# Rank and place of a step's 32 response products in the merged stage of a state-space and spectral mix

## The chip, the cores and the metric

The kernel runs on one core of one Trainium2 chip, as one launch. The metric is the time of the device in microseconds (us); lower is better. Five engines work side by side, each through its own instructions in a fixed order: TensorE (PE in the profile, its weight loads apart as PEld), VectorE (DVE), ScalarE (ACT), GpSimd (POOL) and SyncE (SP, which here only issues DMAs). An engine waits for another by semaphores, and an instruction that waits holds up all that stand behind it on its engine.

## The reference

Two branches work on one input `u` of 2048 positions and 640 channels, and a gate mixes them:

```python
def _A_ref(u, log_A_real, A_imag, C_real, C_imag, log_dt, D_skip):
    P = jnp.exp((A * dt[:, None])[:, :, None] * pos[None, None, :])
    K = 2.0 * jnp.einsum("dn,dnl->dl", C, P).real
    Kf = jnp.fft.rfft(K, L2)
    Uf = jnp.fft.rfft(u_t, L2)
    y = jnp.fft.irfft(Uf * Kf[None, :, :], L2)[:, :, :L]
    return y + u * D_skip[None, None, :]
def _B_ref(x, w_r, w_i):
    X = rfft2(x, axes=(-2, -1)) * (w_r + 1j * w_i)
    return irfft2(X, s=(S, D), axes=(-2, -1))
g = _sigmoid((x * gate_w).sum(-1, keepdims=True))
return g * a + (1 - g) * b
```

Branch a convolves each channel with a response `K` that is a sum over 128 complex modes of exp(pos x mode). Branch b is a filter in the two-dimensional spectrum.

## The kernel before

**Stages.** Every Fourier transform is done by matrix products with tables. In `body`, two streams of code are merged. The first, `ga`, is `phase_a` and the start of `phase_c`: the transform of `u` (products `p_s` in lines 372 and 385, copied out to tiles `t` and `ut`), then the spectral filter of branch b, a pipeline over nine blocks with transposes `p_t` (L557), products `p_d` (L573, L574), elementwise work on DVE (`xx`, `mm`, `zz`, `pm`, `ff`, L580 to L606), products `p_eo` (L618, L619) and `p_i` (L633). The second, `gl`, is `phase_p` and `phase_b`, which build the responses `K`. After both, `phase_d` convolves, gates and stores.

**The responses.** `phase_b` has 40 steps `t`, in batches of five. A position is split into two digits, so that a step's response is a product of two factors `x` and `y`, each a magnitude times a sine or cosine:
- `mags(t)`: three products `p_e` (L700) and three exponentials on ACT (L702) give the magnitudes. The five steps of a batch do this together, because the exponential and the sine each need their own table on ACT.
- `phases(t)`: two PSUM banks of three bf16 products each, `p_p` (L710), give the phases. The tiles of `p_e` and `p_p` share two banks.
- `trig(t)`: one absolute value on DVE (`aq`, L720) and five activations on ACT (L723 to L727) give `sc`, `sx` and `cx`. `sx` and `cx` have one buffer each.
- `prods(t)`: three instructions on DVE write `x` (L734, L735, L736), two on POOL write `y` (L739, L740). `x` and `y` have three buffers each.
- `kgen(t)`: the 32 response products `p_k` (L753), 128 x 32 weights by 128 x 64 columns in fp32, four of them side by side in the array. Each is two matmuls in the trace. After two steps ACT copies the bank to `kt` (L759), and after ten SP stores `kt` to the tensor `k_d` (L761), from which `phase_c` and `phase_d` load it again.

In the code `kgen(t - 3)` comes after `phases(t)` and `trig(t)`, except at the batch's edges, where `kgen` stands between the magnitudes of the next batch:

```python
            if len(pend) > 2:
                yield from kgen(pend.pop(0))
```

**What sets the order.** A scheduler places all instructions, engine by engine, before the run. An instruction's rank is the place at which the code reached it (the two streams are merged by estimated costs), and among the instructions that the scheduler takes to be ready, the one with the best rank is placed. Products of low rank thus fall into the places where others are not yet ready. `tc.issue_after(i)` adds a constraint of order alone: what is traced inside stands behind `i` on `i`'s engine.

## Time and profile before

| what | value |
|---|---|
| median of 3 runs | 561.67 us (560.4 to 561.99) |
| profiled execution, time | 560.56 us |
| its span | 558.8 us |
| PE, DVE, ACT, POOL busy | 516.2, 447.5, 339.8, 273.9 us |
| granted TensorE clock, mean | 0.984 |
| first and last response product | 79.0 and 395.1 us |
| response products' union on PE | 55.5 us of 2560 matmuls |

The responses lie in the stretch from 79 to 395 us, beside the work of the other stream. What counts in a table by stretches is which engine has no idle time left there: only work that leaves that engine can shorten the stretch.

### The profile page before, as it was taken

The numbers are of one execution on the slowest core, as the hardware profiler recorded it, in microseconds if no ns is written. First come the engines' busy times: TensorE is split into PE (matmuls) and PEld (weight loads), VectorE is DVE, ScalarE is ACT, GpSimd is POOL, SyncE is SP. The second block draws the span as 40 slices with busy tenths as digits, with TensorE's granted clock in tenths as the row PEclk, the third lists the DMA queues.
The fourth block names the chain that finished last, engine by engine and source line by source line (L and its number), as shares of the span: only waits on it lengthen the run. The fifth ranks groups of instructions, "written<-read, shape, count | busy, mean of one in ns | idle before, by whom it ended". The sixth has DMA issues, their size and how long they took to land.

```text
span 558.8 us, 16697 instructions
## 1 busy us (share of the span) xinstructions
PE 516.2 (92%) x7124; PEld 394.9 (71%) x7152; DVE 447.5 (80%) x684; ACT 339.8 (61%) x626; POOL 273.9 (49%) x277
## 2 busy tenths in 40 slices
PE   8899899997989899998999989999799999999975
PEld 6789456665857576867777766767787887787741
DVE  5997279479799979999979979876296885977945
ACT  4674677585587689797899786898224223241210
POOL 4993254056246327346257546165163446648433
PEclk9999999999899999999999999999899999999979
DMA  8969233165250331353222132115958989899877
GB/s 322 373 203 347 95 111 110 21 234 187 64 197 17 129 123 60 81 166 128 79 60 71 49 81 95 54 49 190 390 210 267 347 285 354 281 294 316 259 237 265
DMA packets 47697, 100.61 MB, mean 180 GB/s; under 512 B 3492, under 2 KB 32952, under 8 KB 45960
## 3 DMA queue, kind: packets, MB, share of 16 engines
q1 hardware_dynamic: 25176, 67.41, 34.7%
q10 hardware_dynamic: 20080, 22.52, 12.4%
q0 software_dynamic: 2368, 9.64, 5.1%
q8 instruction: 56, 0.92, 0.7%
q14 instruction: 17, 0.14, 0.1%
HBM read 60.22 MB, written 39.65 MB: 179 GB/s over the span
## 4 chain that ended last, share of the span: by engine, by line
PE 37%; DVE 6%; DMA 3%; ACT 3%; issue 1%; ACTq 0%; DVEq 0%; POOL 0%; SPq 0%
PE p_s L372 6%; PE p_s L385 6%; PE p_i L893 5%; PE p_e L172 3%; PE p_p L710 2%; PE p_k L753 2%; PE p_c L972 2%; DMA s_d<-s 2%; PE p_e L700 2%; PE p_i L633 2%; PE p_t L557 2%; PE p_eo L618 2%; PE p_eo L619 1%; PE p_d L573 1%; PE p_d L574 1%
## 5 line engine op out<-in xcount | busy, mean ns | idle before, releaser
L385 PE MATMUL p_s<-t,w 128*64 128x160 f32 x1056 | 90.5, 308 | 4.7 <-ACT ut L420 2.3
L385 PEld LDWEIGHTS p_s<-t,w 128*64 128x64 f32 x1056 | 75.4, 136 | 15.3 <-issue 4.3
L739 POOL TENSOR_TENSOR y<-e,sc 128x512 f32<-128x512 f32 x40 | 53.5, 1339 | 57.3 <-ACT sc L724 42.6
L702 ACT ACTIVATE e<-p_e 128x512 f32<-128x512 f32 x120 | 69.2, 608 | 14.0 <-PE p_e L700 12.7
L710 PE MATMUL p_p<-rp,par 128*128 128x512 bf16 x212 | 63.0, 380 | 8.1 <-ACT sx L726 4.5
L373 ACT COPY t<-p_s 128x512 f32<-128x512 f32 x40 | 24.8, 623 | 63.6 <-PE p_s L372 46.8
L753 PEld LDWEIGHTS p_k<-x,y 128*32 128x32 f32 x2560 | 42.2, 109 | 25.1 <-issue 20.7
L753 PE MATMUL p_k<-x,y 128*32 128x64 f32 x2560 | 55.5, 222 | 0.9 <-DVE x L735 0.8
L740 POOL TENSOR_TENSOR y<-e,sc 128x512 f32<-128x512 f32 x40 | 53.7, 1342 | 0.0
L700 PE MATMUL p_e<-rm,par 96*128 96x512 bf16 x120 | 43.4, 383 | 7.6 <-ACT e L702 4.3
L862 DVE TENSOR_TENSOR ma<-p_s,us 128x640 f32<-128x640 f32 (+1 forms) x36 | 28.2, 783 | 27.7 <-issue 22.0
L736 DVE TENSOR_TENSOR x<-e,cx 128x1024 f32<-128x1024 f32 x40 | 48.4, 1209 | 0.0
L372 PEld LDWEIGHTS p_s<-c,kt 128*64 128x64 f32 x640 | 39.2, 139 | 12.6 <-issue 7.1
L372 PE MATMUL p_s<-c,kt 128*64 128x128 f32 x640 | 44.6, 278 | 3.4 <-issue 2.2
L893 PE MATMUL p_i<-t,w 128*64 128x160 f32 x528 | 43.6, 306 | 3.9 <-POOL t L868 3.6
L895 ACT COPY s<-p_i 128x640 f32<-128x640 f32 x32 | 21.7, 694 | 38.7 <-PE p_i L893 23.4
L868 POOL TENSOR_TENSOR t<-mb 64x320 f32<-64x320 f32 (+1 forms) x36 | 29.9, 832 | 30.5 <-DVE t L868 30.1
L893 PEld LDWEIGHTS p_i<-t,w 128*64 128x64 f32 x528 | 37.4, 139 | 8.8 <-POOL t L868 4.3
L868 POOL TENSOR_TENSOR t<-ma 64x320 f32<-64x320 f32 x32 | 28.3, 886 | 29.9 <-DVE ma L862 28.7
L372 PE MATMUL p_s<-c,u 128*64 128x128 f32 x640 | 40.3, 276 | 0.8 <-ACT ut L420 0.6
L372 PEld LDWEIGHTS p_s<-c,u 128*64 128x64 f32 x640 | 35.3, 136 | 7.4 <-issue 5.3
L710 PEld LDWEIGHTS <-par 128*128 128x128 bf16 x240 | 21.3, 97 | 25.9 <-issue 12.0
(164 smaller groups left out, 1172.6 us busy)
## 6 DMA issues: line engine op xcount, KB each, us to landing
u_d<-ut SPq DMA_DIRECT2D x32, 320.0 KB, 2.8
us<-u_d ACTq DMA_DIRECT2D x16, 640.0 KB, 6.2
s_d<-s ACTq DMA_DIRECT2D x15, 640.0 KB, 9.2
t<-s_d SPq DMA_DIRECT2D x14, 640.0 KB, 6.8
ww<-in_w_l SPq DMA_DIRECT2D x8, 642.0 KB, 5.1
ue<-u_d SPq DMA_DIRECT2D x8, 640.0 KB, 4.2
k_d<-kt SPq DMA_DIRECT2D x4, 1280.0 KB, 4.5
kt<-k_d SPq DMA_DIRECT2D x8, 640.0 KB, 5.6
```

Of the source, the lines that this page charges most:

```text
L372: nc.tensor.matmul(p[64 * ri:64 * ri + 64, j, :], src(i + j), e1[ri], start=True, stop=True)
L385: ins = nc.tensor.matmul(p[64 * j:64 * j + 64, i, 160 * ri:160 * ri + 160], w2[:, x, 64 * ri:64 * ri + 64], t1[:, x // 2 if x < 32 else K0 ...
L700: P.matmul(p[:, :], pars[1][t], rm[:, c:c + 512], start=True, stop=True)
L702: st.exp = S.activation(ef[:, c:c + 512], p[:, :], AF.Exp)
L710: P.matmul(p[:, :], pars[0][t], w, start=i == 0, stop=i == 2)
L736: V.tensor_tensor(out=x[:, 0].rearrange("p d (h j) -> p d h j", h=2), in0=e[:, :, 0:64].rearrange("p d (h j) -> p d h j", h=2), in1=cx.uns ...
L739: G.tensor_tensor(out=y[:, 1], in0=e[:, :, 64:96], in1=sc[:, 0], op=ALU.mult)
L740: G.tensor_tensor(out=y[:, 0], in0=e[:, :, 64:96], in1=sc[:, 1], op=ALU.mult)
L753: P.matmul(st.pb[32 * r:32 * r + 32, o, :], y[:, ri, 4 * qq + JR[r], :], x[:, ri, 4 * qq + JR[r], :], start=t % 2 + qq + 1 - ri == 0, stop ...
L862: V.tensor_tensor(out=ma[:nl, :hn], in0=pv, in1=uu, op=ALU.mult)
L868: return eng.tensor_tensor(out=t2[64 * im:64 * im + 64, o, :], in0=m[l, :hn, 0, :], in1=m[l, :hn, 1, :], op=ALU.add if im else ALU.subtract)
L893: T.mm = P.matmul(p[x:x + 64, i // 2, 160 * (i % 2):160 * (i % 2) + 160], T.w3[:, k0 + h + i, x:x + 64], t2[:, h + i, :], start=True, stop ...
```

## The change

The response products are now placed under two conditions. They stand behind the latest phase product that the code has reached (`st.pp`, by `issue_after`), and their rank is raised by 200 places. Nothing is computed in another way, and no instruction is added or removed.

```diff
@@ phases(t, r)
-                P.matmul(p[:, :], pars[0][t], w, start=i == 0, stop=i == 2)
+                st.pp = P.matmul(p[:, :], pars[0][t], w, start=i == 0, stop=i == 2)
@@ kgen(t)
-        for qq in range(4):
-            o = 4 * (t % 2) + qq
-            for ri in (1, 0):
-                for r in (0, 1, 2, 3):
-                    P.matmul(st.pb[32 * r:32 * r + 32, o, :], y[:, ri, 4 * qq + JR[r], :], x[:, ri, 4 * qq + JR[r], :],
-                             start=t % 2 + qq + 1 - ri == 0, stop=t % 2 * qq == 3 and ri == 0)
+        with after(st.pp), tc.high_priority(offset=200):
+            for qq in range(4):
+                o = 4 * (t % 2) + qq
+                for ri in (1, 0):
+                    for r in (0, 1, 2, 3):
+                        P.matmul(st.pb[32 * r:32 * r + 32, o, :], y[:, ri, 4 * qq + JR[r], :], x[:, ri, 4 * qq + JR[r], :],
+                                 start=t % 2 + qq + 1 - ri == 0, stop=t % 2 * qq == 3 and ri == 0)
```

Below, a run is a row of response products that nothing else interrupts on PE. There are 83 runs before and 37 after; 24 of the 37 hold exactly one step's 32 products. By stretches of the span before, the runs are:

| stretch, us | steps whose products lie there | runs before | runs after |
|---|---|---|---|
| 72 to 111 | 0 to 3 | 14 | 4 |
| 111 to 135 | 4 to 8 | 11 | 4 |
| 158 to 205 | 9 to 13, before also a part of 14 | 11 | 6 |
| 205 to 244 | 14 to 18 | 8 | 4 |
| 244 to 271 | 19 to 23 | 8 | 6 |
| 271 to 323 | 24 to 28 | 12 | 4 |
| 323 to 353 | 29 to 33 | 8 | 5 |
| 353 to 396 | 34 to 39 | 11 | 4 |

On PE, at the end of the first batch (from the last phase product of step 4 on; the rows hold the end of step 1, step 2 and in the second list step 3), before:

```order
L710 MATMUL p_p<-rp,par_526 128x512
L753 MATMUL p_k<-x,y 32x64 x3
L385 MATMUL p_s_1248<-t_805,w_69 64x160 x4
L385 MATMUL p_s_1309<-t_805,w_69 64x160 x2
L372 MATMUL p_s_1315<-c_66,u 64x128 x8
L700 LDWEIGHTS par_1036
L700 MATMUL p_e<-rm,par_1036 128x512
L372 MATMUL p_s_1337<-c_66,u 64x128 x8
L753 MATMUL p_k<-x,y 32x64 x13
```

and now:

```order
L710 MATMUL p_p<-rp,par_526 128x512
L754 MATMUL p_k<-x,y 32x64 x32
L385 MATMUL p_s_1248<-t_805,w_69 64x160 x4
L385 MATMUL p_s_1309<-t_805,w_69 64x160 x2
L754 MATMUL p_k<-x,y 32x64 x36
L372 MATMUL p_s_1315<-c_66,u 64x128 x3
L754 MATMUL p_k<-x,y 32x64 x28
L372 MATMUL p_s_1315<-c_66,u 64x128 x5
```

Steps 2 and 3 moved ahead of the transform's products and of the next batch's magnitudes, and none of step 1 now stands ahead of the phase product.

On PE, in the fifth batch (from the last phase product of step 24 on; `p_k` are here the products of steps 21, 22 and 23, `p_d` those of the filter), before:

```order
L710 MATMUL p_p<-rp,par_2831 128x512
L753 MATMUL p_k<-x,y 32x64 x3
L574 MATMUL p_d<-td,ft 128x161
L573 MATMUL p_d<-td,ft 128x160
L574 MATMUL p_d<-td,ft 128x160
L753 MATMUL p_k<-x,y 32x64 x29
L573 MATMUL p_d<-td,ft 128x161
L574 MATMUL p_d<-td,ft 128x161
L573 MATMUL p_d<-td,ft 128x160
```

and now:

```order
L710 MATMUL p_p<-rp,par_2831 128x512
L754 MATMUL p_k<-x,y 32x64 x32
L573 MATMUL p_d<-td,ft 128x160
L574 MATMUL p_d<-td,ft 128x160
L573 MATMUL p_d<-td,ft 128x161
L754 MATMUL p_k<-x,y 32x64 x32
L574 MATMUL p_d<-td,ft 128x161
L573 MATMUL p_d<-td,ft 128x160
L754 MATMUL p_k<-x,y 32x64 x4
L574 MATMUL p_d<-td,ft 128x160
```

Before, steps 22 and 23 came behind all 16 `p_d` of the block; now 22 comes behind the fifth and the first four products of 23 behind the seventh.

On SP, at the end of the merged stage (`kt` are the responses loaded again, `k_d` the store of the last ten steps, `t3e` the result of the spectral filter, `w_5290` the table `T.w3` that `phase_d` needs for `p_i`), before:

```order
L809 DMA kt<-k_d 128x1280 x3
L1016 DMA w_5290<-in_t_w 128x1408 x3
L761 DMA k_d<-kt 128x2560
L809 DMA kt<-k_d 128x1280
L933 DMA t3e<-s3e_d 128x2560
```

and now:

```order
L810 DMA kt<-k_d 128x1280 x2
L762 DMA k_d<-kt 128x2560
L810 DMA kt<-k_d 128x1280 x2
L934 DMA t3e<-s3e_d 128x2560
L1017 DMA w_5290<-in_t_w 128x1408 x3
```

The store of the responses moved ahead of the third load, and the table's three loads moved behind the fourth `kt` and behind `t3e`. On ACT, the copy of a finished pair of response banks moved ahead of the table load that precedes the exponentials, in the batches that start at steps 5, 20, 25, 30 and 35. DVE and POOL keep the same instructions, with neighbours exchanged. The order of `phase_d` behind its first products is the same but for one place.

## The prediction

> **What bounds the kernel now.** First the page: busy time, the chain that ended last, the response products' group.

> ```profile
> PE 516.2 (92%) x7124; PEld 394.9 (71%) x7152; DVE 447.5 (80%) x684; ACT 339.8 (61%) x626; POOL 273.9 (49%) x277
> PE 37%; DVE 6%; DMA 3%; ACT 3%; issue 1%; ACTq 0%; DVEq 0%; POOL 0%; SPq 0%
> L753 PE MATMUL p_k<-x,y 128*32 128x64 f32 x2560 | 55.5, 222 | 0.9 <-DVE x L735 0.8
> ```

> PE carries most of the chain. An average over stages does not say where, so I read next the busy time by stretches, cut at the bursts of phase products and at the filter's DVE work (columns: stretch, length, PE, PEld, DVE, ACT, POOL, granted clock, DMA share, GB/s).

> ```profile
> 72.00:111.00 39.00, 38.79 (x647) 25.57 (x647) 28.38 (x45) 26.30 (x46) 13.74 (x12) 1.00 0.25 79
> 111.00:135.00 24.00, 23.16 (x428) 15.14 (x434) 20.20 (x37) 16.51 (x28) 13.20 (x11) 1.00 0.61 209
> 135.00:158.00 23.00, 19.36 (x160) 16.52 (x153) 19.66 (x31) 14.57 (x28) 8.05 (x11) 0.85 0.39 119
> 158.00:205.00 47.00, 40.94 (x536) 29.58 (x538) 45.87 (x69) 34.50 (x65) 20.41 (x21) 1.00 0.34 118
> 205.00:244.00 39.00, 38.79 (x482) 29.31 (x484) 35.82 (x55) 34.61 (x68) 20.14 (x22) 1.00 0.25 73
> 244.00:271.00 27.00, 24.77 (x415) 18.96 (x419) 26.16 (x37) 21.78 (x39) 15.98 (x14) 1.00 0.37 125
> 271.00:323.00 52.00, 51.38 (x608) 38.95 (x599) 46.28 (x75) 45.91 (x92) 26.80 (x24) 1.00 0.24 69
> 323.00:353.00 30.00, 26.64 (x437) 19.12 (x441) 27.24 (x36) 23.25 (x43) 15.06 (x11) 1.00 0.25 83
> 353.00:399.00 46.00, 42.14 (x678) 31.24 (x680) 26.88 (x41) 37.46 (x76) 17.84 (x19) 1.00 0.43 156
> ```

> Two kinds alternate. In 72 to 135, 205 to 244, 271 to 323 and most of 353 to 399 PE has almost no idle time (0.21 us of 39 in the first), and DVE has several us: PE sets the pace. In 158 to 205, 244 to 271 and 323 to 353 DVE is the fuller engine (26.16 of 27): PE time saved there shortens nothing.

> **What a run costs on PE.** The timeline of PE, from one start to the next (columns: start, us, engine, line, work, count of matmuls):

> ```profile
> 80.01 0.31 PE L753 MATMUL p_k<-x,y 128*32 128x64 f32 x6
> 80.26 0.82 PE L710 MATMUL p_p<-rp,par 128*128 128x512 bf16 x3
> 81.01 0.97 PE L753 MATMUL p_k<-x,y 128*32 128x64 f32 x52
> 81.92 0.82 PE L710 MATMUL p_p<-rp,par 128*128 128x512 bf16 x2
> ...
> 366.07 0.81 PE L710 MATMUL p_p<-rp,par 128*128 128x512 bf16 x3
> 366.72 1.24 PE L633 MATMUL p_i<-qq,w 128*128 128x320 f32 x4
> ```

> Six matmuls take 80.26 - 80.01 = 0.25 us, 52 take 0.91. So one more costs 0.66 / 46 = 0.0143 us, and a run costs 0.25 - 6 x 0.0143 = 0.164 us whatever its length. The row ahead of a run pays too: three phase products last 0.75 us with responses behind them (80.26 to 81.01) and 0.65 with `p_i` behind (366.07 to 366.72), 0.10 more. One run less is thus worth 0.264 us. The bounds: 0.164 where the neighbour pays nothing, and 0.36 where the fp32 row behind pays as well, as the chain has it:

> ```profile
> 302.37 1.03 PE p_k L753 x64
> 303.40 0.47 PE p_eo L618 x2
> 303.88 0.27 PE p_eo L619 x2
> ```

> (0.47 against 0.27). I take 0.264, since most of the cuts are by bf16 rows, `p_e` and `p_p`, whose rows behind a run show no further surcharge.

> **The change part by part.** It removes no work; it takes away 83 - 37 = 46 runs, 46 x 0.264 = 12.1 us of PE (7.5 to 16.6 by the bounds). By the table of runs:

> - 72 to 111 (10 runs fewer), 111 to 135 (7), 205 to 244 (4), 271 to 323 (8), 353 to 396 (7): 36 runs, 9.5 us, on the engine that sets the pace. This counts.
> - 158 to 205 (5), 244 to 271 (2), 323 to 353 (3): 10 runs, 2.6 us, covered by DVE. I count 0. If DVE's cover were gone they would count in full, hence the lower end.

> What it costs. First, the fillers between the phase products of a burst are gone in the first two batches: a phase product waits for one of two banks, which ACT's sines release.

> ```profile
> 81.22 0.59 ACT L724 ACTIVATE sc<-p_p 128x512 f32<-128x512 f32 x1
> 83.27 0.59 ACT L726 ACTIVATE sx<-p_p 128x512 f32<-128x512 f32 x1
> ```

> Step 3's first bank needs the first of these (step 2), which ends at 81.81; its second bank needs the second, at 83.86. Before, responses of step 0 stood in between. Now PE has ended step 2 by about 80.4 (81.01 before, less two short runs of some 0.3 us), does four transform products, is at step 3 by 81.1 and waits about 0.7 us, and again about 1.2 us for the second bank, though half of this moves with ACT, which gets its inputs earlier. I take 0.9 us for each of the first two batches, 1.8 together; the ends are 0 (ACT keeps up) and 4.5 (nothing of the 17 runs is left there).

> Second, responses of rank 200 higher come before their factors are ready, and what is behind them on PE waits too. The place is the fifth batch, PE, DVE and ACT before:

> ```profile
> 261.24 0.59 PE L710 MATMUL p_p<-rp,par 128*128 128x512 bf16 x2
> 261.77 0.31 PE L753 MATMUL p_k<-x,y 128*32 128x64 f32 x6
> ...
> 267.28 0.67 DVE L735 TENSOR_TENSOR x<-e,sx 128x512 f32<-128x512 f32 x1
> 267.88 1.21 DVE L736 TENSOR_TENSOR x<-e,cx 128x1024 f32<-128x1024 f32 x1
> 271.33 0.48 DVE L580 TENSOR_TENSOR xx<-p_d,bc 128x321 f32<-128x321 f32 x1
> ...
> 269.83 1.28 ACT L702 ACT_TABLE_LOAD   x1
> ```

> From 261.77 PE now does step 21 (1.03), three `p_d` (0.27 each, 0.2 for the switch), step 22 (1.03) and two `p_d` (0.65), and is at step 23's first four products by 265.5. These need L735 of step 23, which the filter's DVE work holds until 267.95. PE stands for 2.4 us, and nine `p_d` behind it. Then four `p_d` and the other 28 products (L736 ends at 269.09) and five `p_d` with two `p_e`: done at about 271.8, which is where PE stood before with nearly the same work done; and DVE wants the `p_d` no earlier than 271.33. So the wait takes the place of a lead, in a stretch where DVE is the bound. What is left over is ACT: the copy of step 23's bank now stands ahead of the table load at 269.83, and ends about 0.5 us later. The eighth batch (step 33) has the same form. 2 x 0.5 = 1.0 us; the ends are 0 and 2 x 2.4.

> Third, the last stretch: the four runs of steps 36 to 39 become two, between the transform's products that PE would do anyway. I take off 0.5 us for waits at adjacent phase products, as before step 37.

> On SP the three loads of `T.w3` go behind the fourth `kt`:

> ```profile
> 388.84 2.25 SPq L1016 DMA_DIRECT2D w<-in_t_w  x3
> 392.00:396.00 4.00, 4.00 (x147) 3.45 (x135) 0.00 (x0) 1.83 (x3) 0.24 (x1) 1.00 1.03 408
> 398.29 0.65 PE L372 MATMUL p_s<-c,kt 128*64 128x128 f32 x7 [2.24 <-issue]
> 415.59 1.31 PE L893 MATMUL p_i<-t,w 128*64 128x160 f32 x16
> ```

> They would be issued near 400, together with `kt` and `t3e`: 128 x (1280 + 2560 + 3 x 1408) fp32 numbers by the order of SP, 4.1 MB; at the 408 GB/s of the second row that is 10 us, so they land by 410, before their first use at 415.59. Cost 0, with up to 3 us if they crowd out other loads. The 2.24 us in which PE waits for nothing visible at full DMA load may go with the calmer traffic; I count 0, with 2.2 us for the lower end. POOL's and DVE's exchanges of neighbours have the same work in total: 0.

> **The sum.** -9.5 + 1.8 + 1.0 + 0.5 = -6.2 us. The profiled execution took 560.56 us (span 558.8), so 554.4. The median of the runs shown is 561.67, 1.1 above the profiled one, and on that scale it is 555.5 us, which I predict.

> **The rivals.** *PE has slack that the stretches hide.* The burst is paced by the single buffers between ACT and DVE, and PE time saved turns into waits:

> ```profile
> ACT sx L726 <- DVE x L735: 15.6, 10, 3.0
> POOL y L739 <- PE p_k L753: 11.0, 7, 3.1
> ```

> Then the 9.5 us shrink to what the phase-product waits leave, 17 runs less 4.5 us (0) in the first batches and half of the 19 others, 2.5 us, less 1.5: about 1 us gained, 560.7. For it: DVE is at 46.28 of 52 in 271 to 323. Against it: 38.79 of 39 in the first stretch. [...]

> *A late response blocks PE.* This is the one on the other side. If the wait for L735 is not made up, at steps 13, 23 and 33, it costs 3 x 2.4 = 7.2 us in place of the 1.0, and an idle PE loses clock: the stretch 135 to 158 holds these two gaps,

> ```profile
> 137.27 0.38 PE L700 MATMUL p_e<-rm,par 96*128 96x512 bf16 x1 [1.42 <-ACT e L702]
> 139.32 2.82 PE L557 MATMUL p_t<-c,fg 128*128 128x128 f32 x12 [1.67 <-POOL fg L540]
> ```

> and a granted clock of 0.85, 0.15 x 23 = 3.45 us lost. With one such spell more: -6.2 - 1.0 + 7.2 + 3.45 = +3.5, 565.1 us. It decides from 7.2 us of waits on. Against it: the `p_d` held up are wanted by DVE only at 271.33. [...]

> *All of it counts.* DVE-bound stretches shorten too, because responses no longer hold up `y` (the 11.0 us above) and the filter begins earlier: -12.1 - 2.2 = -14.3, 547.4. For it speaks the exchange on DVE that puts the filter's first addition ahead of two copies near 135; against it 26.16 of 27.

> *The change does not do what it says.* In the order it does: 24 runs of exactly 32, seven of 36 or 64, and only four steps cut at 4 and 28. I leave it no chance.

> **How the numbers follow.** Forecast (551 to 559) 0.50; all of it 0.16; slack 0.16, a third of it beyond 0.3%; late response 0.18. A measurement of this kernel tells about 0.3% (1.7 us) from no change. Faster 0.50 + 0.16 + 0.05 = 0.71, same 0.11, slower 0.18. The range for 8 in 10 goes from 547.5 (the full gain) to 564.5.

> **What would show it.** Right: the response products' union on PE falls from 55.5 by about 46 x 0.164 = 7.5 to 48 us; PE stays without gaps in 271 to 323; step 23's first products wait for L735 about 2.4 us; the first batch's phase products wait for ACT near 81 and 83. Wrong: PE gaps of more than 7 us in all before response rows, a clock under 0.95 in a stretch that had 1.00, the `phase_d` products `p_i` waiting for `T.w3`, or a union that falls while PE's gaps grow by as much.

## Result: the change makes the kernel slower, and the profile after

The changed kernel takes 564.71 us (median of 10 runs, 561.88 to 568.34), the kernel before 560.98 us beside it: a ratio of 1.008, 95% interval 1.0057 to 1.0104. The forecast was 555.5 us. The profiled execution of the changed kernel took 563.32 us, its span is 561.5.

The page of the changed kernel: busy time, the instruction queue, the response products' group (`kgen`'s product is now line 754).

```profile
PE 511.0 (91%) x7152; PEld 393.2 (70%) x7152; DVE 447.1 (80%) x684; ACT 340.5 (61%) x626; POOL 268.8 (48%) x277
q8 instruction: 56, 0.92, 0.7%
L754 PE MATMUL p_k<-x,y 128*32 128x64 f32 x2560 | 46.1, 224 | 8.4 <-issue 3.7
```

The products' union on PE fell from 55.5 to 46.1 us, and the idle time right before them rose from 0.9 to 8.4 us: of the 9.4 us that the runs saved, 7.5 stand there again as waits. The stretches of the changed kernel show where (same columns and cuts as in the prediction):

```profile
205.00:244.00 39.00, 36.37 (x500) 27.58 (x499) 37.25 (x56) 34.57 (x67) 19.24 (x21) 1.00 0.32 100
...
271.00:323.00 52.00, 49.34 (x586) 38.46 (x585) 45.81 (x71) 45.72 (x88) 22.10 (x22) 1.00 0.28 82
323.00:353.00 30.00, 25.83 (x427) 18.19 (x427) 28.08 (x38) 21.50 (x42) 14.34 (x11) 0.94 0.15 56
353.00:399.00 46.00, 39.20 (x623) 29.03 (x623) 25.56 (x38) 34.58 (x69) 17.46 (x18) 0.96 0.38 132
```

Where PE had 0.2 us of idle time in 39 it now has 2.6, and where it had 0.6 in 52 it has 2.7; the granted clock is below 1.00 in the last two, which had it in full.

To compare kernels whose orders differ I cut the stage at places that all of them pass: its start is the place where DVE reaches step 0's first factor (`x`, L734, at 75.4 us before), then the 33rd and the 257th matmul of `p_eo` (at 197 and 374 us before), then the first product of the transform's second stage in `phase_d`'s data (L385, 399.6 us before). Part A is the first of the three pieces, B the second, C the third. PE's time in a piece is split into waits (no matmul runs), response products, and the rest; each matmul counts from where the one ahead of it ends. All numbers in us, from the profiled executions; the last column is the time at a granted clock of 0.50, below called half clock, in A, B and C.

| kernel | ratio to before, 95% | stage | A | B | C | waits in B | products in B | half clock in A, B, C |
|---|---|---|---|---|---|---|---|---|
| before | 1 | 324.2 | 121.1 | 177.5 | 25.6 | 7.3 | 25.7 | 6.8, 0, 0 |
| changed | 1.008 (1.0057 to 1.0104) | 326.3 | 115.6 | 182.0 | 28.7 | 13.6 | 23.1 | 3.4, 3.4, 3.4 |
| 1: steps 0 to 35 | 1.0013 (0.9977 to 1.005) | 325.1 | 117.4 | 181.6 | 26.1 | 13.3 | 22.6 | 6.8, 3.4, 0 |
| 2: steps 36 to 39 | 1.0042 (1.0004 to 1.0079) | 326.8 | 120.8 | 177.5 | 28.5 | 6.3 | 25.8 | 6.8, 0, 3.4 |
| 3: steps 0 to 23 | 0.9973 (0.9943 to 1.0003) | 321.8 | 117.1 | 178.8 | 25.9 | 8.9 | 24.9 | 6.8, 0, 0.3 |
| 4: order alone | 1.007 (1.0038 to 1.0101) | 328.7 | 120.9 | 181.9 | 25.8 | 11.0 | 24.3 | 13.7, 3.4, 0 |
| 5: half of 24 to 35 left out | 1.0 (0.9972 to 1.0028) | 323.1 | 121.6 | 177.2 | 24.3 | 8.9 | 21.7 | 6.8, 0, 0.5 |
| 6: half of 4 to 13 left out | 1.0016 (0.9986 to 1.0046) | 324.2 | 121.6 | 178.8 | 23.8 | 6.7 | 26.6 | 20.5, 0, 0 |
| 7: one phase product earlier | 1.0231 (1.0199 to 1.0264) | 336.0 | 120.0 | 191.1 | 24.8 | 15.1 | 24.5 | 6.8, 13.7, 0.6 |
| 8: steps 4 to 13 | 0.9961 (0.9935 to 0.9986) | 320.2 | 116.2 | 178.5 | 25.4 | 6.6 | 26.0 | 6.8, 0, 0 |
| 9: kernel 1 and useless products | 1.0005 (0.9971 to 1.004) | 329.5 | 117.8 | 185.3 | 26.5 | 12.9 | 24.4 | 0, 10.2, 0 |
| 10: changed, 32 products more | 1.0006 (0.997 to 1.0043) | 328.2 | 118.7 | 181.9 | 27.5 | 14.6 | 22.6 | 0, 3.4, 3.4 |
| 11: before, 32 products more | 1.0032 (1.0008 to 1.0056) | 325.8 | 120.2 | 178.4 | 27.2 | 7.3 | 26.6 | 6.8, 0, 3.4 |
| 12: kernel 2, 32 products more | 1.0016 (0.9996 to 1.0035) | 325.7 | 120.3 | 178.4 | 27.1 | 7.3 | 26.6 | 3.4, 0, 3.4 |

Part A of one order differs from execution to execution by some 2 us (115.6, 117.4, 117.8 in the changed kernel and kernels 1 and 9, which have the same order there), so an A from one execution is good to about 2 us. B and C repeat better where no half clock falls into them (B is 177.5 in the kernel before and in kernel 2, which has its order there). By the sum of its stretches the prediction had A at -2.7 (-4.5 and 1.8 of costs), B at -3.5 (17 runs less 1.0) and C at 0 (two runs less 0.5). The changed kernel gave -5.5, +4.5 and +3.1. The 8 us between -3.5 and +4.5 in B are the largest part of the error, C is the second. The loss in B lies behind step 24's factors, that is in its last 100 us: the changed kernel is 4.4 us ahead of the kernel before at B's start, 4.6 at those factors, and 0.1 behind at B's end.

The granted clock has to be set apart. In the kernel before, four `p_d` last 1.07 us from 142.36 us, at half clock, and four 0.55 us from 145.03 us, at a clock of 1.00. By this ratio I estimate that a spell of 3.4 us at half clock costs at most 1.7 us of PE's time. The changed kernel has one in each part. The kernel before has 6.8 us in A and none in B and C; its next one begins at 400.45 us, 0.8 us behind the end of C. So up to 1.7 us of the loss in B, and as much in C, are the clock. For all executions that enter the ratios, the time that the clock takes can be estimated from the mean granted clock of each (one less the clock, times the span): 9.0 us in the changed kernel, and in the kernel before 8.2 to 8.9, by its executions beside the other runs. So the changed kernel's loss, 3.7 us by the medians, is not the clock as a whole. Where this estimate bears on an experiment, it stands there.

### The profile page after: what moved, and what is told of

It reads as the page before. It is cut to its first block, busy times and chain, and to the rows that moved or that the text cites. A ratio compares the mean times of both kernels' runs of the same rounds, so it can differ in the third digit from the quotient of the medians.

```text
span 561.5 us, 16740 instructions
## 1 busy us (share of the span) xinstructions
PE 511.0 (91%) x7152; PEld 393.2 (70%) x7152; DVE 447.1 (80%) x684; ACT 340.5 (61%) x626; POOL 268.8 (48%) x277
## 3 DMA queue, kind: packets, MB, share of 16 engines
q10 hardware_dynamic: 20080, 22.52, 12.5%
## 5 line engine op out<-in xcount | busy, mean ns | idle before, releaser
L385 PE MATMUL p_s<-t,w 128*64 128x160 f32 x1056 | 91.2, 308 | 5.5 <-ACT ut L420 3.1
L385 PEld LDWEIGHTS p_s<-t,w 128*64 128x64 f32 x1056 | 76.1, 136 | 16.0 <-issue 4.3
L702 ACT ACTIVATE e<-p_e 128x512 f32<-128x512 f32 x120 | 69.2, 607 | 19.1 <-PE p_e L700 18.2
L739 POOL TENSOR_TENSOR y<-e,sc 128x512 f32<-128x512 f32 x40 | 53.5, 1336 | 45.9 <-ACT sc L724 38.3
L710 PE MATMUL p_p<-rp,par 128*128 128x512 bf16 x240 | 64.3, 379 | 10.1 <-ACT sx L726 5.3
L373 ACT COPY t<-p_s 128x512 f32<-128x512 f32 x40 | 24.8, 622 | 60.8 <-PE p_s L372 40.2
L754 PEld LDWEIGHTS p_k<-x,y 128*32 128x32 f32 x2560 | 39.2, 112 | 22.4 <-issue 15.9
L863 DVE TENSOR_TENSOR ma<-p_s,us 128x640 f32<-128x640 f32 (+1 forms) x36 | 28.2, 783 | 32.9 <-issue 26.1
L754 PE MATMUL p_k<-x,y 128*32 128x64 f32 x2560 | 46.1, 224 | 8.4 <-issue 3.7
L736 DVE TENSOR_TENSOR x<-e,cx 128x1024 f32<-128x1024 f32 x40 | 48.4, 1210 | 0.0
L372 PEld LDWEIGHTS p_s<-c,kt 128*64 128x64 f32 x640 | 39.9, 140 | 10.2 <-issue 6.6
L372 PE MATMUL p_s<-c,kt 128*64 128x128 f32 x640 | 44.4, 278 | 1.8 <-DVE mb L864 1.3
L700 PE MATMUL p_e<-rm,par 96*128 96x512 bf16 x120 | 43.3, 383 | 2.8 <-ACT e L702 2.4
L710 PEld LDWEIGHTS <-par 128*128 128x128 bf16 x240 | 22.1, 97 | 31.5 <-issue 17.8
L372 PE MATMUL p_s<-c,u 128*64 128x128 f32 x640 | 41.3, 278 | 1.4 <-issue 0.7
L372 PEld LDWEIGHTS p_s<-c,u 128*64 128x64 f32 x640 | 36.3, 138 | 8.3 <-issue 6.3
```

The source lines that it names most:

```text
L372: nc.tensor.matmul(p[64 * ri:64 * ri + 64, j, :], src(i + j), e1[ri], start=True, stop=True)
L385: ins = nc.tensor.matmul(p[64 * j:64 * j + 64, i, 160 * ri:160 * ri + 160], w2[:, x, 64 * ri:64 * ri + 64], t1[:, x // 2 if x < 32 else K0 ...
L700: P.matmul(p[:, :], pars[1][t], rm[:, c:c + 512], start=True, stop=True)
L702: st.exp = S.activation(ef[:, c:c + 512], p[:, :], AF.Exp)
L710: st.pp = P.matmul(p[:, :], pars[0][t], w, start=i == 0, stop=i == 2)
L736: V.tensor_tensor(out=x[:, 0].rearrange("p d (h j) -> p d h j", h=2), in0=e[:, :, 0:64].rearrange("p d (h j) -> p d h j", h=2), in1=cx.uns ...
```

## Experiments on where the loss is

**1. The change in steps 0 to 35 alone.**

```diff
-        with after(st.pp), tc.high_priority(offset=200):
+        with (after(st.pp) if t < 36 else nullcontext()), (tc.high_priority(offset=200) if t < 36 else nullcontext()):
```

> The change for steps 0 to 35 alone; the products of steps 36 to 39 stand as before, and so do SP's loads. Theory T (the end of the stage): rows and times up to step 35 are those of the changed kernel, which was 1.2 us ahead of the kernel before at step 39's factors (2.3 us counted from step 0), and then lost 4.4 us up to the first product of the transform's second stage (399.62 before, 402.85 after). Without that loss the kernel is faster than before: ratio 0.996 to 0.998, first product of the second stage at 397.3 to 398.5 us. Rival S (the loss is spread over the stage: long runs make the filter late, and the lead is gone by 385 us whatever stands at the end): ratio 1.001 to 1.006.

Ratio 1.0013, first product of the second stage at 400.20 us: S's numbers, not T's. C is back at 26.1, near before, but B is 4.1 us longer than before, with up to 1.7 us of it by the clock. The loss is not at the end alone.

**2. The opposite part: steps 36 to 39 alone.** The same condition with `t >= 36`.

> The change for steps 36 to 39 alone, which is the opposite part. Theory T: slower than before by the whole loss of the tail, 4.4 us or a little less: ratio 1.005 to 1.008, with most of the first block's transform products behind step 39 and SP's loads of kt behind 395 us, as in the changed kernel. Rival S: ratio 0.999 to 1.002.

Ratio 1.0042, C at 28.5: nearly T's numbers. So both are true: B loses, and so does the end (where a spell at half clock falls into C, too).

**3. Steps 0 to 23 alone.** The same condition with `t < 24`.

> The change for steps 0 to 23 alone. In the changed kernel the lead over the kernel before was 4.6 us at step 24's factors (5.7 us counted from step 0) and 2.1 to 3.2 us from step 29 to step 34. If the order of steps 24 to 35 lost this lead (runs between the filter's products), the lead stays here to the end: ratio 0.990 to 0.993, step 34's factors 4.5 to 5.7 us ahead of before. If another engine or load bounds those stretches whatever the order of p_k (the lead is absorbed), step 34's factors are 2 to 3.5 us ahead, as in the changed kernel, and the ratio is 0.995 to 0.998.

Ratio 0.9973, and step 34's factors 2.6 us ahead: the second reading, a part of the lead is absorbed in B (+1.3). But with the order of before for steps 24 to 35, B is 2.8 us shorter than in kernel 1, which has a spell at half clock there. By the ratios steps 0 to 23 are worth some -1.5 us, steps 24 to 35 some +2, steps 36 to 39 +2.4; each ratio has an interval of about 2 us to either side, and only the last is clear of zero. The clock took 7.1 us in kernel 3's executions and 8.9 in those of the kernel before beside it, which is as much as the whole gain.

**4. The constraint of order alone, without the higher rank.**

```diff
-        with after(st.pp), tc.high_priority(offset=200):
+        with after(st.pp):
```

> The constraint of order alone, without the higher rank: 56 runs, of which the batch edges are cut again, and the last four steps as before. By 0.264 us for a run, 27 runs fewer than before are 7.1 us less on PE, 19 runs more than the changed kernel 5.0 us more. Theory T: faster than before, ratio 0.992 to 0.998, since the tail stands as before. Rival S: with the same whole blocks in the filter's stretches as the changed kernel, ratio 1.000 to 1.006.

Ratio 1.007, outside T and just above S. The 27 runs fewer lowered the union to 50.5 us, and the kernel is slower all the same: 4.4 us more in B, and 17.1 us at half clock instead of 6.8. Over all executions the clock took 12.5 us against 8.9 before: by this estimate it is 3.6 of the 3.9 us by which kernel 4 is slower.

## Experiments on why the middle loses

What is different in B shows in PE's groups from 205 to 378 us (busy, mean ns, then the idle time right before them), before:

```profile
L710 PE MATMUL p_p<-rp,par 128*128 128x512 bf16 x127 | 37.6, 379 | 5.0 <-ACT sx L726 3.0 <-ACT sc L724 1.0 <-issue 0.2
L753 PE MATMUL p_k<-x,y 128*32 128x64 f32 x1336 | 28.7, 222 | 0.0
L557 PE MATMUL p_t<-c,fg 128*128 128x128 f32 (+3 forms) x64 | 8.7, 266 | 0.0
```

in the changed kernel:

```profile
L710 PE MATMUL p_p<-rp,par 128*128 128x512 bf16 x135 | 36.6, 378 | 7.2 <-ACT sx L726 3.7 <-ACT sc L724 3.5
L754 PE MATMUL p_k<-x,y 128*32 128x64 f32 x1356 | 24.7, 224 | 3.3 <-DVE x L735 2.3 <-POOL y L739 0.7 <-issue 0.3
L557 PE MATMUL p_t<-c,fg 128*128 128x128 f32 (+3 forms) x60 | 8.1, 266 | 0.6 <-DVE qq L625 0.6
```

and with the change in steps 0 to 23 alone:

```profile
L710 PE MATMUL p_p<-rp,par 128*128 128x512 bf16 x140 | 38.3, 379 | 5.2 <-ACT sx L726 3.2 <-ACT sc L724 1.9
L754 PE MATMUL p_k<-x,y 128*32 128x64 f32 x1408 | 28.5, 221 | 1.4 <-DVE x L735 0.7 <-POOL y L739 0.7
```

The products got 4.0 us cheaper (28.7 to 24.7), and the waits of these three groups grew by 6.1 (5.0 to 11.1). One of the places, PE's timeline at the first phase products of a batch, before:

```profile
324.62 1.04 PE L557 MATMUL p_t<-c,ff 128*128 128x128 f32 x8
325.59 0.97 PE L753 MATMUL p_k<-x,y 128*32 128x64 f32 x50
326.87 0.81 PE L710 MATMUL p_p<-rp,par 128*128 128x512 bf16 x2 [0.31 <-ACT sc L724]
```

and in the changed kernel:

```profile
321.45 1.04 PE L557 MATMUL p_t<-c,ff 128*128 128x128 f32 x8
323.69 0.81 PE L710 MATMUL p_p<-rp,par 128*128 128x512 bf16 x3 [1.21 <-ACT sc L724]
```

From the start of the eight transposes to the phase product it is 2.25 us before and 2.24 now. The 50 matmuls stood in a wait for ACT's sine; with them gone the wait is bare, and where they were put instead they take PE time again. So the theory for B, F below: response products of low rank cover waits that no idle time shows. Five runs bear on it.

**5. Half the products of steps 24 to 35 left out.** In the kernel before:

```diff
-            for ri in (1, 0):
+            for ri in ((1,) if 24 <= t < 36 else (1, 0)):
@@ the matmul's last argument
-                             start=t % 2 + qq + 1 - ri == 0, stop=t % 2 * qq == 3 and ri == 0)
+                             start=t % 2 + qq + 1 - ri == 0, stop=t % 2 * qq == 3 and (ri == 0 or 24 <= t < 36))
```

> The kernel before without 16 of the 32 response products of each of the steps 24 to 35 (the half with the imaginary factors is left out), 192 products or some 5.4 us of PE time at 0.9 us for 32. Theory F (cover): between 271 and 378 us PE works on the response products while it waits for ACT and DVE, so taking them away uncovers waits; the stage from step 0's factors to the second stage's first product gets shorter by less than 1.5 us, and PE's gaps in it grow by 3 us or more. Rival P (PE sets the pace there, as the prediction had it): shorter by 4 to 5.4 us, gaps as before.

The stage got 1.1 us shorter and the ratio is 1.0. The rival P, which is the prediction's own view, is out: it asked for 4 to 5.4 us. Busy time of the engines from 271 to 378 us, before and then here (columns as above):

```profile
271.00:378.00 107.00, 102.25 (x1247) 74.74 (x1244) 92.41 (x141) 92.71 (x182) 53.19 (x46) 1.00 0.23 71
```

```profile
271.00:378.00 107.00, 100.12 (x906) 69.99 (x896) 93.28 (x142) 93.27 (x183) 53.80 (x46) 1.00 0.22 70
```

In B the products got 4.0 us less, the waits 1.6 more and the other rows 2.1 more, so that B is 0.3 us shorter. F is met by half: its 3 us of waits are not reached (0.9 over the stage). That the other rows take longer when fewer response products stand between them was not expected, and its cause is not shown.

**6. The same in steps 4 to 13.**

> The same half left out in steps 4 to 13 of the kernel before, 160 products or 4.5 us. This is where the changed kernels gained 3.3 to 5.1 us. Theory F, if PE sets the pace in 111 to 167 us and DVE from there on: shorter by 2 to 4 us. If the gain of the changed kernels there was not PE time but the better order of other work: shorter by less than 1 us.

The stage is as long as before (324.2) and the ratio 1.0016. From 115 to 205 us, before and then here:

```profile
115.00:205.00 90.00, 79.47 (x1077) 58.71 (x1083) 82.83 (x129) 62.04 (x115) 40.74 (x43) 0.96 0.40 134
```

```profile
115.00:205.00 90.00, 78.67 (x738) 57.44 (x738) 81.15 (x128) 62.50 (x115) 38.88 (x43) 0.89 0.38 128
```

160 products fewer, and PE is busy for 0.8 us less: the granted clock is 0.89 instead of 0.96, with 20.5 us at half clock in the stage. The profiled execution, at 565.11 us, is the longest of the ten. Over all ten the clock took 10.3 us, against 8.2 in the kernel before beside them. That the emptier PE is the reason is not shown, and whether PE's time alone would have shortened A can't be read from this run.

**7. Behind the phase product of the step before the latest**, in steps 0 to 35, rank as in the change.

```diff
@@ phases(t, r)
-                st.pp = P.matmul(p[:, :], pars[0][t], w, start=i == 0, stop=i == 2)
+                st.tp = t
+                st.pps[t] = P.matmul(p[:, :], pars[0][t], w, start=i == 0, stop=i == 2)
@@ kgen(t)
-        with after(st.pp), tc.high_priority(offset=200):
+        with (after(st.pps.get(st.tp - 1)) if t < 36 else nullcontext()), (tc.high_priority(offset=200) if t < 36 else nullcontext()):
```

> As the kernel with the change in steps 0 to 35, but the products stand behind the phase product of the step before the latest, so that they can be placed ahead of the latest one; 54 runs. Theory F: the 1.2-us waits of the phase products near 241 and 322 us are covered again, and the sum of PE's gaps is 2 to 5 us less than with the change in steps 0 to 35 (27.1); 15 runs more cost 3 us at 0.2 us for a run, so the ratio stays at 0.996 to 1.003. Rival (the waits come from the higher rank, not from the place behind the latest phase product): gaps as with the change in steps 0 to 35, 26 to 28 us, ratio 1.004 or more.

F's numbers did not come: 1.0231, with 29.2 us of waits in the stage. The rival's ratio (1.004 or more) did, with more waits than its 26 to 28. The groups from 205 to 378 us (`p_p` is line 712 here, `p_k` 756, `x` 737):

```profile
L712 PE MATMUL p_p<-rp,par 128*128 128x512 bf16 x120 | 32.9, 379 | 5.9 <-ACT sx L728 3.0 <-ACT sc L726 3.0
L756 PE MATMUL p_k<-x,y 128*32 128x64 f32 x1280 | 24.1, 225 | 2.8 <-DVE x L737 2.5 <-POOL y L741 0.3
...
L557 PE MATMUL p_t<-c,fg 128*128 128x128 f32 (+3 forms) x60 | 9.8, 298 | 4.1 <-DVE qq L625 3.7 <-ACT ft L562 0.3
```

The freed products did not cover the waits of the phase products, which fell only from 6.9 us in kernel 1 to 5.9, and the transposes wait now (4.1 us). The waits in B grew with the constraint alone (11.0 in kernel 4) and with the rank and a looser constraint (15.1 here), from 7.3 before; I read this as the early place opening the waits, by rank or by constraint. The rest of the loss is the clock: 13.7 us at half clock fall into B, where before none did, and over all executions it took 15.2 us against 8.2.

**8. Steps 4 to 13 alone.** The condition of experiment 1 with `4 <= t < 14`.

> The change for steps 4 to 13 alone, where the changed kernels gained: their lead at step 15's factors is 3.1 to 4.7 us, and the kernels with the change in steps 0 to 23 had lost 0.9 to 1.2 us by step 5, which is not lost here. If the lead lasts where the order behind it is that of before: ratio 0.990 to 0.994, and step 39's factors 4 to 5.5 us ahead. If a later stretch absorbs a lead whatever its order (1.3 us went between 265 and 317 us with the change in steps 0 to 23): 2.5 to 4 us ahead, ratio 0.993 to 0.996.

This is the second reading: step 39's factors are 3.9 us ahead, counted from step 0, and the ratio, 0.9961, lies just above its 0.996. The stage is 4.0 us shorter: A gives 4.9, and B takes back 1.0. The clock has no part in it (6.8 us at half clock in A in both, 8.1 and 8.2 us by the estimate). This version is faster than both kernels. Nearly all of these steps lie ahead of B.

**9. Useless work in the waits.** Kernel 1 with 40 products that are thrown away, of low rank and unbound:

```diff
+        for r in (0, 1, 2, 3) * (10 if t in (34,) else 0):
+            P.matmul(st.pb[32 * r:32 * r + 32, 0, :], y[:, 1, JR[r], :], x[:, 1, JR[r], :], start=True, stop=True)
```

> The kernel with the change in steps 0 to 35, and in addition 40 response products whose result is thrown away (repeats of step 34's first four), of low rank and bound to no phase product: they fall where step 34's own products stood before, ahead of the phase products of steps 36 and 37. They are 0.9 to 1.5 us of useless work on PE. Theory F with the clock: the waits of 0.2 to 0.7 us near 367 to 370 us are covered, the spell at half clock at 370 us (3.4 us long, 1.7 us lost) does not come, and step 39's factors are earlier, not later, than with the change in steps 0 to 35: 0.9 us behind before there, now 0 to 2 us ahead; ratio 0.996 to 1.000. Rival (the loss there is work on PE or on DVE's path): step 39's factors 1 to 1.5 us later still, 1.9 to 2.4 us behind before, ratio 1.002 to 1.006.

The timeline of PE in kernel 1, and then with the useless products (line 750):

```profile
366.47 0.81 PE L710 MATMUL p_p<-rp,par 128*128 128x512 bf16 x3 [0.31 <-ACT sc L724]
...
370.11 2.67 PE L710 MATMUL p_p<-rp,par 128*128 128x512 bf16 x6 [0.74 <-ACT sc L724]
```

```profile
371.28 0.65 PE L750 MATMUL p_k<-x,y 128*32 128x64 f32 x32
371.87 0.82 PE L710 MATMUL p_p<-rp,par 128*128 128x512 bf16 x3
```

The piece between the 225th and the 257th matmul of `p_eo` holds 1.8 us more of response products than in the changed kernel (2.8 against 1.0) and 1.4 us less of waits (0.4 against 1.8), and it lasts exactly as long: 17.10 us in both. In kernel 1, with a spell at half clock in it, it is 18.27; in the kernel before, 15.98. The ratio, 1.0005, is not above kernel 1's, though just outside the range that F gave; its interval of 2 us to either side can't tell 1 us of work. In the profile the products in these waits are free, even useless ones: PE does not set the pace there. But covering the waits did not bring the 15.98 us back either. The bare waits show that PE is not the bound; they are not shown to be what makes B longer than before. The expected earlier factors of step 39 can't be seen: this execution had 10.2 us at half clock at 348 us.

## Experiments on the end of the stage

PE's timeline at the end, in the changed kernel and in kernel 2 (steps 36 to 39 alone):

```profile
385.48 3.16 PE L372 MATMUL p_s<-c,kt 128*64 128x128 f32 x46
388.97 1.73 PE L754 MATMUL p_k<-x,y 128*32 128x64 f32 x95 [0.33 <-POOL y L740]
393.92 1.12 PE L754 MATMUL p_k<-x,y 128*32 128x64 f32 x33 [3.22 <-issue]
394.97 7.20 PE L372 MATMUL p_s<-c,kt 128*64 128x128 f32 x106
```

```profile
387.07 1.64 PE L754 MATMUL p_k<-x,y 128*32 128x64 f32 x99
392.65 1.07 PE L754 MATMUL p_k<-x,y 128*32 128x64 f32 x29 [3.94 <-issue]
```

In the middle of steps 38 and 39 PE stops for 3 to 4 us with nothing in the trace that it waits for ("issue"). The kernel before has a stop too, of 2.24 us, later:

```profile
394.26 1.10 PE L753 MATMUL p_k<-x,y 128*32 128x64 f32 x64
395.29 0.76 PE L372 MATMUL p_s<-c,kt 128*64 128x128 f32 x9
398.29 0.65 PE L372 MATMUL p_s<-c,kt 128*64 128x128 f32 x7 [2.24 <-issue]
```

In each of these a packet of the instruction queue is under way during the stop. The DMA queues from 390.7 to 393.9 us in the changed kernel (packets, MB, share of the 16 engines), and the data alone from 388.7 to 392.7 in kernel 2:

```profile
q10 hardware_dynamic: 76, 0.31, 23.4%
q8 instruction: 1, 0.02, 1.9%
```

```profile
q10 hardware_dynamic: 256, 1.15, 72.8%
```

There are 56 packets in all, 0.92 MB (the `q8` row above), or 16 KB each and one for some 255 instructions of PE: the trace has 7152 matmuls and as many weight loads. Kernel 5, with 384 matmuls and 384 weight loads fewer, has 53 packets: three fewer for 768 instructions, or 256 for one. So the theory, I, inferred from these rows, none of which names what PE waits for: PE has run out of fetched instructions. A shift of their number tells. In both kernels a spell at half clock begins as the stop ends (from 393.84 to 397.25 us in the changed kernel). The clock at the end of the stage, before and then in the changed kernel:

```profile
394.50:399.62 5.12, 2.20 (x80) 1.63 (x68) 0.00 (x0) 1.68 (x3) 0.00 (x0) 1.00 1.03 374
```

```profile
394.97:402.85 7.88, 7.21 (x110) 6.96 (x106) 0.00 (x0) 4.85 (x8) 0.24 (x1) 0.86 0.69 254
```

**10. The changed kernel with 128 instructions more on PE**, at step 6, all else in the same order.

```diff
+                    for r in (0, 1, 2, 3) * (8 if t == 6 and qq == 0 and ri else 0):
+                        P.matmul(st.pb[32 * r:32 * r + 32, o, :], y[:, ri, 4 * qq + JR[r], :], x[:, ri, 4 * qq + JR[r], :], start=True, stop=True)
```

> The changed kernel with 32 more response products ahead of step 6's (repeats of its first four), nothing else moved. These are 64 matmuls and 64 weight loads, 128 instructions on PE. In the changed kernel PE stops for 3.22 us after 95 of the 128 matmuls of steps 38 and 39, with nothing to be seen that it waits for, while a packet of the instruction queue is under way. If PE has run out of fetched instructions there, the stop belongs to a number of instructions and comes 64 matmuls earlier in the program, after some 31 of the 128 (20 to 45). If it belongs to the place (a wait for y, a bank or a buffer that the trace does not name), it stays after some 95.

PE's timeline here (`p_k` is line 756):

```profile
392.64 2.02 PE L756 MATMUL p_k<-x,y 128*32 128x64 f32 x128
394.59 1.96 PE L372 MATMUL p_s<-c,kt 128*64 128x128 f32 x31
398.03 2.18 PE L372 MATMUL p_s<-c,kt 128*64 128x128 f32 x36 [1.47 <-issue]
```

Neither number came: steps 38 and 39 run through, and the stop is 33 + 31 = 64 matmuls later, not earlier. With 64 matmuls and 64 weight loads more ahead of it, it has moved by 256 instructions in all, one packet's worth. That the place counts in blocks of 256 is thus a reading after this run; experiments 11 and 12 test it. From the first transform product to the second stage it is 17.3 us instead of 19.9, and the kernel with 1 us of useless work more has a ratio of 1.0006 instead of 1.008. Of these 4.1 us C shows 1.2 in the profiled executions (28.7 and 27.5), and the clock, which took 6.6 us in kernel 10 and 9.0 in the changed kernel, would be 2.4 by the estimate; so the ratio's gain is not the stop's alone. (The profiled A is 3.1 us longer, about 1 us of it the useless products, the rest as A varies.)

**11. Control: the kernel before with the same 128 instructions more**, at step 16.

> The kernel before with 32 more response products ahead of step 16's (128 more instructions on PE, some 1 us of useless work), nothing else moved; the control of the two shifted kernels. Theory I (the stop of PE near the end of the stage is a late fetch of instructions, and how late depends on their number ahead): the kernel before has its own stop of 2.24 us among the transform's products; it may move or shrink, but the time from the first of these products to the second stage stays at 17 us or a little below, and the ratio is 0.997 to 1.004. Rival N (128 more instructions help any order, by something else): ratio 0.990 to 0.996.

```profile
393.86 0.35 PE L755 MATMUL p_k<-x,y 128*32 128x64 f32 x9
396.45 1.56 PE L755 MATMUL p_k<-x,y 128*32 128x64 f32 x55 [2.23 <-issue]
```

Here the stop is after 9 matmuls of step 39 instead of after all 64 and 9 of the transform: 64 matmuls earlier, exactly the 128 instructions put ahead, and as long as before (2.23 us). It belongs to the count of instructions, not to the work. The ratio, 1.0032, says that more instructions are no help by themselves (N is out); the time from the first transform product to the second stage is 18.7, more than I's 17, since a spell at half clock now falls into it.

This control says one thing more. Its useless products stand at 222 us, inside B, and from there on everything is 0.9 us later, which is their own length (products in B 26.6 instead of 25.7), while the waits in B stay at 7.3. Kernel 12 has the same. There PE does set the pace, as the prediction had it for 205 to 244: F holds where experiments 5 and 9 tested it, behind 271 us, and not for all of B.

**12. The tail alone, shifted by the same 128.**

> The change for steps 36 to 39 alone, as in the second experiment, with the same 32 more products ahead of step 16's. Theory I: the stop inside the products of steps 38 and 39 (3.94 us in the second experiment) is gone or below 2 us, the time from the first transform product to the second stage is 17 to 18 us instead of 19.9, and the ratio falls from 1.0042 to 0.997 to 1.002. Rival (the order of the tail costs by itself, because the transform's products stand behind step 39): the time stays at 19 to 20 us and the ratio at 1.004 to 1.009.

```profile
387.76 2.12 PE L756 MATMUL p_k<-x,y 128*32 128x64 f32 x128
389.80 2.18 PE L372 MATMUL p_s<-c,kt 128*64 128x128 f32 x35
394.26 5.81 PE L372 MATMUL p_s<-c,kt 128*64 128x128 f32 x71 [2.28 <-issue]
```

The stop left the response products (29 + 35 = 64 matmuls later, as in kernel 10) and takes 2.28 us, less than 3.94 but above the 2 that I expected. Ratio 1.0016; the 18.5 us from the first transform product to the second stage are half a microsecond above I's range, with a spell at half clock among them, as in kernel 11. The intervals of kernels 2 and 12 overlap, so the ratios alone do not part them; the stop's place does. Against the control with the same number of instructions (562.53 us) the tail order takes 561.62: placing steps 36 to 39 in rows shows no cost of itself.

The packet's times settle more. All fourteen profiles have this stop near the end of the stage, from 0.6 us (kernel 6) to 3.9, and in all of them PE goes on 2.3 to 2.6 us after the packet of the instruction queue has begun; the packet itself takes 0.9 to 1.2 us. It begins 0.2 us ahead of the stop in the kernel before, 0.8 us into the stop in the changed kernel and 1.6 us into it in kernel 2, and 0.9 us ahead in kernel 10. By these times, how long PE stops is how late this packet begins against PE's work. The late packet is worth 1.0 us in the changed kernel (3.22 against 2.24) and 1.7 in kernel 2; up to 1.7 us more of the loss in C are clock. Why the packet begins when it does is not shown: data took 23% of the DMA engines during the stop in the changed kernel and 73% in kernel 2, and both stop.

## Why the prediction was wrong, step by step

- *A run costs 0.264 us on PE.* The union fell by 9.4 us for 46 runs, 0.20 us each (0.24 in kernel 1, 0.25 in kernel 3), with 48 forecast and 46.1 measured. So the first term, 0.164, was low. The neighbour's 0.10 lies in other rows and can't be read from the union; the price was of the right size.
- *"36 runs, 9.5 us, on the engine that sets the pace. This counts."* This is the step that failed. I read a stretch without idle time on PE as one in which PE sets the pace. Of the 36 runs 17 lie in B, 4.5 us, and 13 of these behind 271 us, 3.4 us. There PE's time does not count. Experiment 5 takes 4.0 us of response products out, and B gets 0.3 us shorter; experiment 9 adds 40 useless products to a piece, which lasts as long. PE was full because response products of low rank had been placed into its waits for ACT and DVE: 0.6 us of idle time in 52 was a cover, not a bound. In the changed kernel the runs saved 2.6 us of products in B, and the waits there grew by 6.3. In 205 to 244 PE does set the pace (experiment 11), but the four runs fewer gained nothing there either: the idle time grew by 2.4 us, and the lead is 4.7 us at step 15's factors and 4.6 at step 24's. That B became 4.5 us longer, and did not just stay as it was, is explained in part only: up to 1.7 us are the spell at half clock, and the bare waits are where the rest stands, not a shown cause. The busy share of PE's weight loads does not part the stretches that gained from the others: it is 75% in 271 to 323 (38.95 of 52), where nothing was gained, and 63% in 111 to 135 (15.14 of 24), among the steps whose new order did gain.
- *The stretch from 158 to 205 counted 0, the first two batches cost 1.8.* Right in the details: step 3's banks wait 0.42 and 1.18 us (0.7 and 1.2 forecast). Part A gained more than its 2.7 us: 3.3 to 5.5 in the changed kernel and kernels 1 and 9.
- *Step 23's first products wait 2.4 us, and nothing hangs on it; 1.0 for the late copies.* They wait 0.70 us; step 13's wait 1.22, step 33's 1.59. The late copies can't be told apart in the traces. A spell at half clock follows the longest of these waits (below).
- *The last stretch costs 0.5.* C is 3.1 us longer. The 2.24-us stop was in the profile, and I gave it to the load on the DMA engines and a possible gain; it goes with a packet of the instruction queue and keeps to a count of instructions (experiments 10 to 12), and in the new place it became 3.22. Up to 1.7 us more are the spell at half clock behind it.
- *`T.w3` late on SP costs 0.* Right: from 405 to 480 us `p_i` waits 0.5 us in all, for DVE.
- *The rival "a late response blocks PE", 565.1 us, 0.18.* It gave the time to 0.4 us, by luck. Two of its signs came: more than 7 us of gaps ahead of response rows (8.4), and a clock under 0.95 in a stretch that had 1.00 (0.94 in 323 to 353). But the waits for factors are 4.5 of the 8.4, not 7.2 (3.5 for `x`, 1.0 for `y`); 3.2 are the stop, which the rival does not have. Its loss of clock by an idle PE rests on one stretch, 135 to 158 us, and other waits do not bear it out: there the spell begins at 137.62 us, ahead of the gap of 1.67 us (from 137.64), and two waits of 1.4 us in the same kernel, at 252 and 332 us, have a granted clock of 1.00 behind them.

## What to carry to other kernels

An engine without idle time is not yet the bound when low-rank work fills its waits: before counting a saving there, ask what would stand in the filler's place, and leave some filler out, or add useless filler, to measure it, stretch by stretch: 32 useless products cost their full 0.9 us at 222 us, and 40 cost nothing near 371. Change the order part by part, and keep it where the part alone gains (here steps 4 to 13, 0.4% faster, though leaving half their products out gained nothing), and leave the filler elsewhere. When a change of order moves a tail by a few microseconds, shift it by half a packet's instructions (128 of 256 here) before giving the loss to the order, and compare the granted clock piece by piece.

## What the runs showed of the hardware

**The same wait is followed by half clock or isn't.** Step 33's first products wait 1.59 us in the changed kernel, in kernel 1 and in kernel 9:

```profile
345.71 0.32 PE L754 MATMUL p_k<-x,y 128*32 128x64 f32 x8 [1.59 <-DVE x L735]
```

```profile
345.85 0.32 PE L754 MATMUL p_k<-x,y 128*32 128x64 f32 x8 [1.59 <-DVE x L735]
```

```profile
346.24 0.32 PE L756 MATMUL p_k<-x,y 128*32 128x64 f32 x8 [1.59 <-DVE x L735]
```

and the clock from 340 to 360 us is 0.91, 1.00 and 0.74 in this order:

```profile
340.00:360.00 20.00, 18.22 (x271) 13.99 (x272) 15.58 (x22) 12.64 (x25) 4.86 (x5) 0.91 0.11 38
```

```profile
340.00:360.00 20.00, 18.11 (x278) 14.04 (x278) 16.77 (x25) 13.72 (x28) 4.86 (x5) 1.00 0.11 38
```

```profile
340.00:360.00 20.00, 18.29 (x250) 12.41 (x250) 12.79 (x16) 10.53 (x20) 4.82 (x5) 0.74 0.06 21
```

That is 3.4, 0 and 10.2 us at half clock; every spell that lies whole in these stages is a multiple of 3.4 us. The spell begins 0.3 us behind the wait in the changed kernel and 1.8 us behind it in kernel 9; that the wait brings it on is not shown.
